# Softmax sums of three head pairs collected in one PSUM bank, one reciprocal for the three, and a new order of calls

## The chip, the core and the metric

The kernel runs on one core of a Trainium2 chip. The metric is the device time of one execution in microseconds (us): the median of several runs, 689.25 us for the kernel before.

## The reference

Attention with rotary positions, followed by a gated feed-forward layer, all in fp32:

```python
def _attn_ref(q, k, v):                      # 4 batches, 8 heads, 576 positions, 64 wide
    ...
    scores = scale * np.matmul(q_rot, k_rot.transpose(0, 1, 3, 2))
    scores = scores - np.max(scores, axis=-1, keepdims=True)
    attn = np.exp(scores)
    attn = attn / (np.sum(attn, axis=-1, keepdims=True) + 1e-09)
    return np.matmul(attn, v).astype(np.float32)

def _moe_ref(x, w_gate, w_val, w_out):       # 2304 x 512, 512 x 1536 twice, 1536 x 512
    gate = 1.0 / (1.0 + np.exp(-(x @ w_gate)))
    val = x @ w_val
    return (gate * val @ w_out).astype(np.float32)
```

`x` is the attention's output with the heads side by side. The feed-forward weights arrive as 64-bit floats.

## The kernel before

**Tiling.** The 8 heads of a batch go in 4 pairs (128 partitions), the 576 query positions of a batch in two halves of 256 and 320 (`HALVES`). A half of a batch passes through attention, then through `hidden` (12 blocks f of the hidden width; line 922 holds its matmuls, which need the attention output `xt` of all four pairs) and then `project` (line 958). fp32 numbers are mostly carried as two fp16 numbers, a high part and a remainder; a scale goes with each.

**Preparation.** At the start the weights are decoded from 64-bit words: `w_in_chunk` for 12 chunks (two exponent and low-bit steps, lines 476 to 484, a join on VectorE, line 488, then high parts and remainders; for six chunks, `VIA_PE`, TensorE makes the remainders with a scaled identity, line 529), and `w_out_decode` and `w_out_split` for the output weights. `values0_split` splits the values of batch 0.

**Batch 0, first half.** This half of 256 queries has its own path, for which the change is made. `keys_queries` turns q and k: TensorE multiplies by a 128x128 constant `turned` (line 639; it lies in the first quarter of the buffer `obuf[1]`), VectorE does the rest (lines 641 to 646). `front` computes scores directly, takes their row maxima (line 771) and brings these into row form. `back` then computes the scores transposed, with keys on the partitions, in five blocks j; ScalarE takes the exponential (line 818). `weigh` (line 822) multiplies, for each j and each of the two heads, the exponentials by the raw fp32 values into the single PSUM bank `v_ps` ("pv") and by a block of ones into a bank of the pool m ("sums"), so that each of the 64 rows of a head holds that head's sums; line 830 is the matmul of both. The end of `back`, per pair, is:

```python
op("ACT", ..., [U], [K], lambda E: A.activation(t(), sums()[:, 0:n], AF.Copy, bias=1e-9))      # line 839
op("DVE", ..., [], [K], lambda E: V.reciprocal(t(), t()))                                      # line 840
op("DVE", ..., ["pv"], [K], lambda E: V.tensor_tensor(                                         # line 841
    out=t(), in0=v_ps[:, 0:n], in1=t(), op=ALU.mult))
```

followed by a high part on ScalarE (line 464), a remainder (line 470) and a maximum (line 845) on VectorE.

**Pools.** PSUM holds two double banks s for scores, the bank pv, and three banks m. SBUF has three buffers p32, three th (the hidden blocks use them) and two p16.

**The order.** `Plan` collects every operation with a rank, an engine or several possible ones, and what it reads and writes; `order` plays it through with its own cost functions and, on each engine, takes the ready operation of the lowest rank; `emit` writes the instructions in that order. Nothing is decided on the chip. Operations enter through 269 calls (`at`), and three tables have one entry per call: `SHIFT` is added to the ranks of a call, `LEAD` to those of its loads, and `SIDE` places its movable operations (`alt`, line 401; `high`, line 407): 0 puts all on their first engine, 1 each first of two on the second engine, 2 all. High parts and low-bit decodes go to ScalarE or VectorE; the rope's two full-width steps per pair of batch 0 to VectorE or GpSimd, the six smaller ones per pair of later batches to GpSimd or VectorE.

## Time and profile before

| | us |
|---|---|
| median of 3 runs (lowest, highest) | 689.25 (688.71, 689.66) |
| the profiled execution | 686.14 |
| its span (first to last instruction) | 684.3 |
| TensorE matmul busy in the span | 645.9 (94%) |
| VectorE busy | 536.8 (78%) |
| ScalarE busy | 391.1 (57%) |
| GpSimd busy | 35.5 (5%) |

Busy shares are averages over stages with different limits. In the first stage, some 110 us, weights are decoded and batch 0 is prepared; later the hidden and output matmuls fill TensorE while the attention of the next batch runs beside them.

### The profile page before, as it was taken

The numbers are of one execution on the slowest core, as the hardware profiler recorded it, in microseconds if no ns is written. First come the engines' busy times: TensorE is split into PE (matmuls) and PEld (weight loads), VectorE is DVE, ScalarE is ACT, GpSimd is POOL, SyncE is SP. The second block draws the span as 40 slices with busy tenths as digits, with TensorE's granted clock in tenths as the row PEclk, the third lists the DMA queues.
The fourth block names the chain that finished last, engine by engine and source line by source line (L and its number), as shares of the span: only waits on it lengthen the run. The fifth ranks groups of instructions, "written<-read, shape, count | busy, mean of one in ns | idle before, by whom it ended". The sixth has DMA issues, their size and how long they took to land.

```text
span 684.3 us, 13000 instructions
## 1 busy us (share of the span) xinstructions
PE 645.9 (94%) x4922; PEld 428.7 (63%) x4922; DVE 536.8 (78%) x1306; ACT 391.1 (57%) x825; POOL 35.5 (5%) x33
## 2 busy tenths in 40 slices
PE   4798978999899999999999999999999999999997
PEld 2444546775466756886776555677885568767645
DVE  4999989999999998899998997597887774543200
ACT  4988889787746576665665545334545662612210
POOL 0000000001011010300001312000000000000000
PEclk9999999999999999999999999999999999999999
DMA  9854437898886588699367798422536661400010
GB/s 351 340 188 149 159 124 179 195 232 195 179 207 130 99 206 192 137 175 212 88 138 180 172 217 188 128 66 58 96 87 114 152 125 32 102 1 1 1 44 33
DMA packets 172669, 97.11 MB, mean 142 GB/s; under 512 B 152896, under 2 KB 161600, under 8 KB 170816
## 3 DMA queue, kind: packets, MB, share of 16 engines
q1 hardware_dynamic: 172608, 96.29, 57.2%
q8 instruction: 38, 0.62, 0.4%
q14 instruction: 23, 0.19, 0.1%
HBM read 40.83 MB, written 4.72 MB: 67 GB/s over the span
## 4 chain that ended last, share of the span: by engine, by line
PE 45%; DVE 30%; DMA 14%; issue 6%; ACT 3%; SPq 1%; POOL 1%; DVEq 0%; ACTq 0%; POOLq 0%
PE m L922 26%; PE m L958 9%; DMA pt<-p 7%; DVE p L470 6%; PE pv L871 4%; DVE p L737 4%; PE s L714 4%; DVE wo L488 2%; DMA stk<-sw 2%; DMA qk<-in_qk_dram 1%; DVE p L466 1%; DVE m L771 1%; DMA xt<-in_v_dram 1%; DVE gt L470 1%; DVE p L840 1%
## 5 line engine op out<-in xcount | busy, mean ns | idle before, releaser
L922 PE MATMUL m<-xt,w 128*128 128x256 f16 (+1 forms) x2304 | 294.8, 286 | 1.2 <-ACT xt L464 0.9
L922 PEld LDWEIGHTS <-w 128*128 128x128 f16 x2304 | 222.9, 98 | 63.7 <-issue 7.7
L958 PE MATMUL m<-wo,gt 128*128 128x512 f16 (+1 forms) x684 | 147.1, 368 | 1.1 <-DVE wo L470 1.1
L742 ACT ACTIVATE p<-p,st 128x576 f32<-128x576 f32 x128 | 98.7, 771 | 60.5 <-DVE p L737 53.4
L470 DVE SCALAR_TENSOR_TENSOR p<-p,st,p 128x576 f16<-128x576 f32 x128 | 107.1, 864 | 14.3 <-ACT p L464 13.9
L958 PEld LDWEIGHTS <-gt 128*128 128x128 f16 x684 | 66.0, 98 | 69.1 <-issue 4.3
L928 ACT ACTIVATE th<-m,gsc 128x320 f32<-128x320 f32 (+1 forms) x96 | 47.3, 494 | 82.2 <-PE m L922 78.6
L737 DVE TENSOR_SCALAR_CACHE_REDUCE p<-s,q_e 128x576 f32<-128x576 f32 x108 | 86.4, 810 | 4.1 <-PE s L714 3.6
L932 DVE SCALAR_TENSOR_TENSOR th<-th,m 128x320 f32<-128x320 f32 (+1 forms) x96 | 42.9, 448 | 39.8 <-PE m L922 38.5
L464 ACT ACTIVATE p<-p,st 128x576 f16<-128x576 f32 x91 | 66.9, 764 | 12.4 <-DMA pt<-p 6.7
L714 PE MATMUL s<-stk 128*128 128x288 f16 (+1 forms) x480 | 66.1, 287 | 4.5 <-DVE p L737 4.4
L871 PE MATMUL pv<-pt,v 128*64 128x320 f16 (+3 forms) x840 | 60.9, 290 | 2.1 <-DMA pt<-p 2.1
L714 PEld LDWEIGHTS <-stk 128*128 128x128 f16 (+1 forms) x480 | 41.5, 100 | 23.6 <-issue 12.0
L871 PEld LDWEIGHTS <-v 128*64 128x64 f16 (+1 forms) x840 | 43.3, 109 | 19.9 <-issue 16.2
L470 DVE SCALAR_TENSOR_TENSOR gt<-th,c_s,gt 128x320 f16<-128x320 f32 (+1 forms) x96 | 49.0, 512 | 8.0 <-ACT gt L464 7.3
L464 ACT ACTIVATE gt<-th,c_s 128x256 f16<-128x256 f32 (+1 forms) x50 | 26.1, 523 | 33.5 <-DVE th L932 29.1
L464 ACT ACTIVATE o<-m,o_s 128x512 f32<-128x512 f32 (+1 forms) x17 | 11.2, 657 | 37.4 <-PE m L958 37.3
L652 POOL TENSOR_TENSOR qk<-qk,tab 128x576 f32<-128x576 f32 x7 | 11.3, 1621 | 279.4 <-DMA qk<-in_qk_dram 209.1
L742 ACT ACTIVATION_READ_ACCUMULATOR p<-p,st 128x1 f32 x128 | 23.9, 187 | 0.0
L466 DVE TENSOR_SCALAR p<-p,st 128x576 f16<-128x576 f32 x37 | 21.0, 576 | 3.8 <-DMA pt<-p 3.5
L464 ACT ACTIVATE xt<-pv 128x320 f16<-128x320 f32 (+1 forms) x28 | 11.3, 405 | 21.2 <-PE pv L871 21.1
L663 ACT ACTIVATE sink<-qk 128x576 int8<-128x576 f32 x24 | 16.3, 680 | 11.8 <-DVE qk L656 5.6
(146 smaller groups left out, 652.3 us busy)
## 6 DMA issues: line engine op xcount, KB each, us to landing
wo<-in_w_dram SPq DMA_DIRECT2D x11, 1024.0 KB, 4.9
qk<-in_qk_dram SPq DMA_DIRECT2D x12, 576.0 KB, 5.5
sw<-in_qk_dram SPq DMA_DIRECT2D x12, 576.0 KB, 4.2
xt<-in_wo_dram SPq DMA_DIRECT2D x12, 512.0 KB, 3.8
stk<-sw SPq DMA_DIRECT2D x24, 216.0 KB, 3.6
stk<-sw SPq DMA_DIRECT2D x72, 72.0 KB, 2.8
out_dram<-o SPq DMA_DIRECT2D x15, 256.0 KB, 2.6
xt<-in_v_dram SPq DMA_DIRECT2D x3, 1152.0 KB, 7.3
```

Source lines behind the costliest of these rows:

```text
L464: A.activation(o, src, AF.Copy, scale=scale)
L466: E.tensor_scalar(out=o, in0=src, scalar1=scale, scalar2=1.0, op0=ALU.mult, op1=ALU.mult)
L470: V.scalar_tensor_tensor(out=o, in0=src, scalar=scale, in1=hi, op0=ALU.mult, op1=ALU.subtract)
L663: op("ACT", c_act(S) + 0.09, rank, [X[m]], ["sink", M], lambda E, m=m: A.activation(sink, x[:, m], AF.Abs, accum_out=q_m[:, k, m:m + 1]))
L714: T.matmul(o[:, c, 0:288], lhsT=q[:, rows:rows + width], rhs=kk[:, c * 288:c * 288 + 288], start=(m == 0), stop=(m == 1))
L737: lambda E, h=h, c=c: V.tensor_scalar(out=prs[c]().rearrange("p (c n) -> p c n", c=2), in0=h()[:, :, 0:288], scalar1=down, scalar2=None, o ...
L742: lambda E, c=c: A.activation(prs[c](), prs[c](), AF.Exp, bias=st[:, k, 0, c:c + 1], scale=-1.0, accum_out=st[:, k, 1, c:c + 1]))
L871: T.matmul(v_ps[64 * e:64 * e + 64, 0:n], lhsT=v16[hs, p, a, g, :], rhs=pt[z][hs, c * 9 + g, 0:n], start=(first and m == 0), stop=(last an ...
L922: T.matmul(m()[:, 0:n], lhsT=w16[:, f, g, a, cc, :], rhs=x[:, cc, c, c0:c0 + n], start=(k == 0), stop=(k == 11))
L928: op("ACT", c_act(n), rank - 0.05, [m, ("gsc", b, f)], [r], lambda E, m=m: A.activation(t(), m()[:, 0:n], AF.Tanh, scale=gsc[:, b, f:f + 1]))
L932: op("DVE", c_dve(n, psum=True), rank - 0.05, [m], [r], lambda E, m=m: V.scalar_tensor_tensor(out=t(), in0=t(), scalar=1.0, in1=m()[:, 0:n ...
L958: T.matmul(m()[:, 0:w], lhsT=gt[:, f, a, c0:c0 + 128], rhs=wo16[:, f, x, c:c + w], start=(f == 0 and k == 0), stop=(f == NF - 1 and k == 2))
```

## The change

`back` gets groups: the pairs 0, 1 and 2 of the first half form one, pair 3 stands alone and keeps the old ending. In the group, the three pairs' sums go into the same bank: the block of ones is replaced by a 64-column window of `hot` (zeros with one column of ones, in the second quarter of `obuf[1]`), so that pair p's sums land on row p of each head's 64 rows. Each pair's product in pv is copied by ScalarE into a th buffer. After the third pair the bank is copied once and its reciprocal taken once; then, per pair, two fp32 matmuls with a broadcast column of the identity spread the pair's row over 64 rows in a bank of m, VectorE multiplies the copy by it, and the split and maximum follow as before (`split`; its high part may now go to VectorE, but all the calls concerned have side 0). `front` and `back` also learn the second half, which `ACROSS = ()` leaves unused.

The cut diff:

```diff
+ACROSS = ()
+GROUPS = ((0, (0, 1, 2)), (0, (3,)))
...
+    hot = obuf[1][:, 128:256]
...
-    def front(p, z, rank):
+    def front(p, i, z, rank):
...
+    groups = {}
+
+    def back(p, i, z, rank):
 
         kT, qT = qk0[p][:, 0], qk0[p][:, 1]
         R = [("stk", m) for m in range(8 * p, 8 * p + 8)] + [("mr", z), ("obuf", 0)]
-        n = HALVES[0][1]
-        w = p % 2
+        c0, n = HALVES[i]
+        w = i or p % 2
         pp = pT[w]
-        sums, U = m_place()
+        pairs = next(g for h, g in GROUPS if h == i and p in g)
+        G = groups.setdefault((i, pairs), {"left": len(pairs), "raw": {}})
+        first = G["left"] == len(pairs)
+        G["left"] -= 1
+        last = not G["left"]
+        if first:
+            G["sums"] = m_place()
+        sums, U = G["sums"]
+        alone = len(pairs) == 1
...
-                        T.matmul(o[es, 0:n], lhsT=ones[hs, 0:64] if one else early[hs, 3 * p + g // 3, 64 * (g % 3):64 * (g % 3) + 64],
-                                 rhs=pp[hs, at0:at0 + n], start=(j == 0), stop=(j == 4), skip_group_check=True)
+                        w_t = early[hs, 3 * p + g // 3, 64 * (g % 3):64 * (g % 3) + 64]
+                        if one:
+                            w_t = ones[hs, 0:64] if alone else hot[hs, 63 - p:127 - p]
+                        T.matmul(o[es, 0:n], lhsT=w_t, rhs=pp[hs, at0:at0 + n], start=(j == 0 and (first or not one)),
+                                 stop=(j == 4 and (last or not one)), skip_group_check=True)
         for js in ((0, 1), (2, 3, 4)):
-            mm(len(js) * 0.0035 * n, rank - 0.02, [("pt", w, j) for j in js] + [("v32", p)], ["pv", U],
+            mm(len(js) * 0.0035 * n, rank - 0.02, [("pt", w, j) for j in js] + [("v32", p), ("obuf", 1)], ["pv", U],
                lambda js=js: weigh(js), mode="C")
-        K = lease("p32")
+
+        def split(p, t, T0):
+            x = xt[0][:, p, :, c0:c0 + n]
+            X, Z = ("xt", 0, p, i), ("xm", 0, i)
+            high(n, rank - 0.02, [T0, ("vs", 0)], [X], x[:, 0], t, v_s[:, 0:1])
+            op2(c_dve(n, two=True), rank - 0.02, [T0, ("vs", 0)], [X], lambda E: rest(x[:, 1], t(), v_s[:, 0:1], x[:, 0]))
+            op("DVE", c_dve(n), rank, [X], [Z], lambda E: V.tensor_reduce(
+                out=xm[:, 0, i, p:p + 1], in_=x[:, 0], axis=AX.X, op=ALU.max, apply_absolute_value=True))
+        K = lease("p32") if last else None
         t = lambda: K()[:, 0:n]
-        x = xt[0][:, p, :, 0:n]
-        X, Z = ("xt", 0, p, 0), ("xm", 0, 0)
-        op("ACT", c_act(n) - 0.11, rank - 0.02, [U], [K], lambda E: A.activation(t(), sums()[:, 0:n], AF.Copy, bias=1e-9))
-        op("DVE", 0.1 + 0.0061 * n, rank - 0.02, [], [K], lambda E: V.reciprocal(t(), t()))
-        op("DVE", c_dve(n, psum=True), rank - 0.02, ["pv"], [K], lambda E: V.tensor_tensor(
-            out=t(), in0=v_ps[:, 0:n], in1=t(), op=ALU.mult))
-        op("ACT", c_act(n), rank - 0.02, [K, ("vs", 0)], [X], lambda E: scaled(A, x[:, 0], t(), v_s[:, 0:1]))
-        op2(c_dve(n, two=True), rank - 0.02, [K, ("vs", 0)], [X], lambda E: rest(x[:, 1], t(), v_s[:, 0:1], x[:, 0]))
-        op("DVE", c_dve(n), rank, [X], [Z], lambda E: V.tensor_reduce(
-            out=xm[:, 0, 0, p:p + 1], in_=x[:, 0], axis=AX.X, op=ALU.max, apply_absolute_value=True))
+        if last:
+            op("ACT", c_act(n) - 0.11, rank - 0.02, [U], [K], lambda E: A.activation(t(), sums()[:, 0:n], AF.Copy, bias=1e-9))
+            op("DVE", 0.1 + 0.0061 * n, rank - 0.02, [], [K], lambda E: V.reciprocal(t(), t()))
+        if alone:
+            op("DVE", c_dve(n, psum=True), rank - 0.02, ["pv"], [K], lambda E: V.tensor_tensor(
+                out=t(), in0=v_ps[:, 0:n], in1=t(), op=ALU.mult))
+            split(p, t, K)
+            return
+        raw = G["raw"][p] = lease("th")
+        op("ACT", c_act(n) - 0.11, rank - 0.03, ["pv"], [raw], lambda E: A.activation(raw()[:, 0:n], v_ps[:, 0:n], AF.Copy))
+        if last:
+            for q in pairs:
+                f, F = m_place()
+                r = G["raw"][q]
+                def spread(f=f, q=q):
+                    for e in range(2):
+                        T.matmul(f()[64 * e:64 * e + 64, 0:n], lhsT=ident[:, 64 * e + q:64 * e + q + 1].to_broadcast([128, 64]),
+                                 rhs=t(), start=True, stop=True)
+                mm(0.00175 * n, rank - 0.02, [K, "ident"], [F], spread, mode="C")
+                op("DVE", c_dve(n, psum=True), rank - 0.02, [F], [r], lambda E, f=f, r=r: V.tensor_tensor(
+                    out=r()[:, 0:n], in0=f()[:, 0:n], in1=r()[:, 0:n], op=ALU.mult))
+                split(q, lambda r=r: r()[:, 0:n], r)
...
+        G.memset(hot, 0.0)
+        G.memset(hot[:, 63:64], 1.0)
...
-            for k, g in ((0, front(p, p % 2, t)), (1, back(p, p % 2, t + step))):
+            for k, g in ((0, front(p, 0, p % 2, t)), (1, back(p, 0, p % 2, t + step))):
```

The tables `SHIFT`, `SIDE` and `LEAD` are replaced as a whole; their 269 calls are the same. The sides that change among the calls of batch 0 and batch 1, with the operations that change engine:

| call | side | moves |
|---|---|---|
| keys_queries batch 0, pair 1 | 0 to 1 | first rope step, the multiply of 1,152 columns, VectorE to GpSimd |
| values0_split pair 2 | 1 to 0 | high part, VectorE to ScalarE |
| w_in_chunk 0 | 0 to 2 | two half-size low-bit decodes, two high parts, two scaled identities to VectorE |
| w_in_chunk 1 | 1 to 2 | a high part and a scaled identity to VectorE |
| w_in_chunk 4, 10 | 1 to 2 | a high part each to VectorE |
| w_in_chunk 5 | 1 to 0 | low-bit decode and a high part to ScalarE |
| w_in_chunk 9 | 0 to 1 | low-bit decode and a high part to VectorE |
| w_in_chunk 11 | 2 to 1 | a high part to ScalarE |
| w_out_decode 0, 10, 11 / 8 | 0 to 1 / 1 to 0 | low-bit decode (512 columns) to VectorE / ScalarE |
| w_out_split 0, 7, 8 / 3, 5 | 0 to 1 / 1 to 0 | high part to VectorE / ScalarE |
| attention of batch 1 | several | 8 high parts to VectorE, 7 to ScalarE |

In batch 2, eight high parts net of the attention and two of the values move from ScalarE to VectorE, in batch 3 three net of the attention to VectorE and four of the values to ScalarE; rope work of the pairs moves both ways. By the ranks of the loads SyncE issues weight chunk 2, `turned` and the identity, then the tables and pair 0's q and k; before, it was chunk 2, the tables, pair 0's q and k, `turned`, the identity. The last call in rank is `project` of batch 3, tile 3 (before, tile 1).

## Rows read from the trace of the kernel before

**Rows 1.** PE, PEld, DVE, ACT, POOL busy us by stretch; then granted clock, DMA share, GB/s.

```profile
0.00:10.00 10.00, 1.18 (x3) 0.93 (x4) 1.92 (x2) 4.45 (x9) 1.21 (x12) 1.00 0.82 315
...
40.00:110.00 70.00, 60.27 (x428) 32.58 (x429) 68.14 (x168) 61.65 (x133) 0.00 (x0) 0.98 0.49 166
110.00:200.00 90.00, 84.45 (x656) 56.45 (x654) 86.96 (x222) 68.57 (x151) 7.43 (x4) 1.00 0.87 198
200.00:400.00 200.00, 196.78 (x1628) 136.72 (x1627) 187.29 (x460) 121.32 (x260) 21.61 (x15) 1.00 0.74 162
400.00:680.70 280.70, 278.38 (x2129) 189.25 (x2127) 165.71 (x410) 110.97 (x227) 5.28 (x3) 1.00 0.36 81
```

**Rows 2.** The chain that ended last, 60 to 104 us: start us, us, what.

```profile
65.72 1.66 DVE p L840
...
67.98 0.61 DVE wo L481
...
77.65 0.40 DVE w L466
78.05 1.66 DVE p L840
...
88.95 1.66 DVE p L840
...
92.21 0.95 PE pv L830 x4
...
94.01 0.85 PE pv L830 x4
...
96.71 0.43 PE pv L830 x4
...
99.05 1.75 DVE p L840
```

**Rows 3.** Waits of TensorE and VectorE, 40 to 110 us: total us, times, longest.

```profile
PE pv L830 <- DVE p L841: 1.6, 2, 1.3
...
DVE p L840 <- ACT p L839: 1.8, 1, 1.8
```

**Rows 4.** The stretches around pair 3's sums, columns as above.

```profile
90.00:92.00 2.00, 0.94 (x8) 0.39 (x4) 2.00 (x5) 1.40 (x4) 0.00 (x0) 1.00 0.74 301
...
93.00:94.00 1.00, 1.00 (x8) 0.62 (x6) 1.00 (x3) 1.00 (x3) 0.00 (x0) 0.50 0.00 0
```

**Rows 5.** Groups by line, 0 to 110 us: busy us, mean ns | idle before.

```profile
L464 ACT ACTIVATE w<-wo,w_s 128x512 f16<-128x512 f32 x15 | 11.1, 771 | 2.3 <-DVE w_s L432 2.0 <-DVE vm L591 0.3
...
L839 ACT ACTIVATE p<-m 128x256 f32<-128x256 f32 x4 | 1.5, 382 | 1.7 <-PE m L830 1.7
...
L644 DVE TENSOR_TENSOR stk<-stk,tab 128x1152 f32<-128x1152 f32 x4 | 5.4, 1348 | 0.0
...
L466 DVE TENSOR_SCALAR v<-gt,v_s 128x576 f16<-128x576 f32 x3 | 2.3, 802 | 0.0
...
L470 DVE SCALAR_TENSOR_TENSOR p<-p,st,p 128x576 f16<-128x576 f32 x2 | 1.6, 810 | 0.0
...
L466 DVE TENSOR_SCALAR ids<-ident,w_s 128x128 f32<-128x128 f32 x4 | 1.0, 253 | 0.0
```

**Rows 6.** Timeline of TensorE and SyncE, one row each.

```profile
97.50 0.19 PEld L830 LDWEIGHTS pv<-pt,gt 64*64 64x64 f32 x4 [0.39 <-issue]
...
2.84 0.44 SPq L996 DMA_DIRECT2D ident<-in_const_dram  x1
```

**Rows 7.** Timeline of GpSimd and of VectorE, around 163 us.

```profile
162.76 2.34 POOL L654 TENSOR_TENSOR sw<-sw,tab 128x576 f32<-128x576 f32 x1 [18.44 <-DMA sw<-in_qk_dram]
...
205.01 1.40 POOL L654 TENSOR_TENSOR sw<-sw,tab 128x576 f32<-128x576 f32 x1 [15.04 <-DMA sw<-in_qk_dram]
...
163.75 1.96 DVE L470 SCALAR_TENSOR_TENSOR p<-p,st,p 128x576 f16<-128x576 f32 x1
```

**Rows 8.** Group of the attention splits on VectorE, 200 to 400 us, columns as in rows 5.

```profile
L466 DVE TENSOR_SCALAR p<-p,st 128x576 f16<-128x576 f32 x18 | 9.9, 556 | 0.4 <-DMA pt<-p 0.4
```

More of the change, by code (lines that the diff above doesn't have):

```diff
@@ L760, in front @@
         M = ("m2", z)
[L761 to L762 removed]
+        for x, t in enumerate(((0, 1), (2, 3, 4))[i]):
+            for c in range(2 if t < 4 else 1):
                 k = lease("s")
                 def direct(t=t, c=c, k=k):
[L766 to L772 removed]
+                    for cc in ((c,) if t < 4 else (0, 1)):
+                        for e in range(2):
+                            hs = slice(64 * e, 64 * e + 64)
+                            w = 128 if t < 4 else 64
+                            o = k()[:, e, 0:288] if t < 4 else k()[hs, cc, 0:288]
+                            T.matmul(o, lhsT=qT[hs, 128 * t:128 * t + w], rhs=kT[hs, 288 * cc:288 * cc + 288],
+                                     start=True, stop=True)
+                mm(0.48, rank, R, [k], direct, mode="R" if t < 4 else "Q")
+                o = m2[:, z, x, c] if t < 4 else m2[:, z, x, :, 0]
+                op("DVE", c_dve(S, psum=True), rank - 0.01, [k], [M], lambda E, k=k, o=o: V.tensor_reduce(
+                    out=o, in_=k()[:, :, 0:288], axis=AX.X, op=ALU.max))
                 yield
[L774 to L775 removed]
+        q = 3 if i else 2
+        a, b, c = (cb[:, z, 0:q, :, r] for r in range(3))
+        y = mx[:, z, 0:q]
         W = [M, ("cb", z)]
[L777 removed]
+        tiny(rank - 0.01, [], W, lambda: V.tensor_tensor(out=y, in0=m2[:, z, 0:q, 0], in1=m2[:, z, 0:q, 1], op=ALU.max), port=True)
         tiny(rank - 0.01, [], W, lambda: V.tensor_copy(a, y), port=True)
@@ L787, in turn_up @@
                          start=True, stop=True)
-        n = HALVES[0][1]
-        mm(0.3, rank - 0.02, [("cb", z), "nid"], [Z], turn_up)
+            for e in range(2 * i):
+                hs = slice(64 * e, 64 * e + 64)
+                T.matmul(ps()[hs, 256:320], lhsT=cb[hs, z, 2, 0], rhs=nid[hs, hs], start=True, stop=True)
+        n = HALVES[i][1]
+        mm(0.3 + 0.3 * i, rank - 0.02, [("cb", z), "nid"], [Z], turn_up)
         op("ACT", c_act(n) - 0.11, rank - 0.02, [Z], [("mr", z)], lambda E: A.activation(mr[z][:, 0:n], ps()[:, 0:n], AF.Copy))
-    def back(p, z, rank):
+    groups = {}
+    def back(p, i, z, rank):
         kT, qT = qk0[p][:, 0], qk0[p][:, 1]
         R = [("stk", m) for m in range(8 * p, 8 * p + 8)] + [("mr", z), ("obuf", 0)]
-        n = HALVES[0][1]
-        w = p % 2
+        c0, n = HALVES[i]
+        w = i or p % 2
         pp = pT[w]
-        sums, U = m_place()
+        pairs = next(g for h, g in GROUPS if h == i and p in g)
[7 more added lines that the diff above has]
+        alone = len(pairs) == 1
         for j in range(5):
@@ L811, in across @@
                     keys = slice(64 * e + 128 * j, 64 * e + 128 * j + 128) if j < 4 else (slice(512, 576), slice(0, 64))[e]
-                    T.matmul(o, lhsT=kT[hs, keys], rhs=qT[hs, 0:n], start=False, stop=True)
+                    T.matmul(o, lhsT=kT[hs, keys], rhs=qT[hs, c0:c0 + n], start=False, stop=True)
             mm(0.00215 * n, rank, R, [k], across, mode="R" if j < 4 else "Q")
@@ L1034, in attend0_rest @@
             t = lo + p * step
+            if p in ACROSS:
+                for k, g in ((0, front(p, 1, p % 2, t)), (0.5, back(p, 1, p % 2, t + 0.5 * step))):
+                    for n in range(6):
+                        at(t + step * (k + n / 12), next, g, None)
+                continue
             at(t - 0.4 * step, values0_split, p, t - 0.4 * step)
```

13 lines of the change are left out of this document (1 added, 12 removed), and 68 rows, old and new, of tables (LEAD, SHIFT, SIDE).

## The prediction, made before the changed kernel was run

> **What bounds the kernel now.** I read the stretches first. From 400 us to the last matmul TensorE does nothing but work, and from 200 to 400 us it is idle for 3.2 us of 200, so a gain has to come from the time before. There TensorE idles 9.7 us of the 70 from 40 to 110 and 5.5 of the 90 from 110 to 200, while VectorE is busy 68.1 of 70 and 87.0 of 90 [rows 1]. VectorE's queue sets the pace of the first 110 us, and ScalarE (61.7 of 70) is close behind.
>
> The chain of waits says what is in that queue. All four reciprocals of batch 0's first half lie on it: 1.66 us for each of pairs 0 to 2 and 1.75 for pair 3, 6.7 us together [rows 2]. Then, at 92.21, the chain leaves VectorE: the weighing matmuls of pair 3 (line 830) had to wait until pair 2's product (line 841) had emptied the single bank pv, and line 841 stands behind pair 2's reciprocal. TensorE lost 1.6 us in two such waits [rows 3]. Worse, after that idling its granted clock is 0.50, the lower of its two levels (1.2 GHz), from 93 to 94 us [rows 4], and each step of pair 3's weighing takes 0.85 us where the later ones take 0.43 [rows 2]. VectorE in turn idles 1.8 us before the last reciprocal, waiting for pair 3's sums [rows 3]. So pair 3 is the gate: no hidden matmul of batch 0 can finish before its product.
>
> **The change part by part.** *Reciprocals.* Of four, two go (pairs 0 to 2 share one). On the queue each costs what the chain gives it, so 2 x 1.66 = **-3.3 us** of VectorE. The three products stay, from a PSUM bank times SBUF as before.
>
> *The bank pv.* It is now emptied by a ScalarE copy of the size of line 839's, 0.38 us [rows 5], and no longer by a product that waits for a reciprocal. Pair 3's weighing need not wait for pair 2's reciprocal: **-1.6 us** of wait. With that idling gone I also expect the higher clock: four steps at 0.85 instead of 0.43 cost 4 x 0.42 = **-1.7 us**. ScalarE gets three such copies and loses two of line 839's, +0.38 us net, which I cost at nothing because it loses far more below; without that cover it is 0.38.
>
> *The spread.* Three times two fp32 matmuls of 256 columns, each pair like one step of line 830, 0.43 us: 1.3 us, and entering the mode once costs 0.39 us of issue [rows 6]; 1.7 in all. It is nothing if they fall into the 9.7 us in which TensorE idles, 1.7 if they stand in front of pair 3's weighing or the hidden matmuls. I take **+0.4**, the entry alone, as the rows nearest to it show TensorE idle 1.06 of 2 us just before 92 [rows 4]. A bank of the pool m is held from pair 0's first weighing to pair 2's last, and three th buffers until the three products; nobody else needs th before pair 3 is done, and the bank is costed in a rival.
>
> *The start.* GpSimd sets two more small memsets, and SyncE now issues both 64 KB constants ahead of the tables and the first q and k, which TensorE's first work waits for; before, ident came after all of these [rows 6]. 64 KB at 315 GB/s [rows 1] is **+0.2 us**. Should SyncE wait for the memsets, the queue still has the 1 MB weight chunk to move meanwhile.
>
> *The sides.* The table of sides moves work between engines, and here the change takes back much of what it gives. Priced by queue time (a row's duration less the 0.08 by which it overlaps with the next: 1.66 for the reciprocal's 1.74), up to the gate: the weight chunks bring VectorE two half-size bit decodes (0.35 each, estimated as somewhat over half of a whole one's 0.61), five high parts net (0.40 each) and three scaled identities (0.18 each, from 253 ns), and one whole decode comes for one that goes [rows 2, 5]: 0.7 + 2.0 + 0.5 = +3.2. One w_out decode: +0.35. One value split leaves (802 ns): -0.7. One rope multiply of 1,152 columns leaves for GpSimd (1,348 ns): -1.3 [rows 5]. With the reciprocals VectorE's queue stands at -3.3 + 3.2 + 0.35 - 0.7 - 1.3 = **-1.7 us** up to the gate, and it has 1.8 us of idling to give besides. ScalarE loses 0.77 us with each high part [rows 5], for five of them 3.9.
>
> A GpSimd multiply is not free for VectorE. At 163.75 an operation of VectorE with two SBUF inputs, issued while GpSimd multiplied, took 1.96 us instead of 0.81 [rows 5, 7]. GpSimd needed 1.40 to 2.34 us for 576 columns [rows 7], so 2.8 to 4.7 for 1,152 is my estimate. I take no cost, since VectorE has reductions and products from PSUM in its queue then, and keep the other end for a rival. The Trainium skill, GPSIMD Engine Reference, section Specifications, says that GpSimd shares its SBUF interfaces with VectorE and contends with its two-input instructions; by that rule the -1.3 could become a loss, and row 163.75 agrees.
>
> *After the gate.* Two w_out decodes in and one out (+0.35), three high parts of w_out in and two out and one of the last weight chunk out (0), one attention split more in batch 1 (+0.45): 0.8 us on a VectorE that has 3.0 us idle in 90 [rows 1]. Between 0 and 0.8 I take **+0.4**.
>
> *The order.* All 269 calls get new shifts. Which instruction follows which can't be read off the table, so it gets no term; its bounds are the 5.5 us that TensorE still idles from 110 to 200 and, on the other side, as much new idling as VectorE's tightest stretch allows.
>
> **The sum.** The gate comes earlier by the smaller of two: VectorE can give 1.7 + 1.8 = 3.5, TensorE's side of pair 3 gives 1.6 + 1.7 = 3.3. So -3.3 + 0.4 + 0.2 + 0.4 = **-2.3 us**. The profiled execution took 686.14 us (span 684.3 and 1.84 around it), 3.1 less than the median of the runs, 689.25; I expect a profiled execution of 683.8 and a median of **687.0**. What a measurement can tell from no change is 0.2%, 1.4 us.
>
> **Rivals.** *More than that.* The order fills TensorE's idling from 110 to 200 as well: half to all of 5.5 us on top, 681.5 to 684.3. For it: ScalarE, the second tightest engine, is relieved by about 4 us. Against: VectorE is busy 97% there and gets 0.8 us more. 0.18.
>
> *Nothing measurable.* Pair 3 gets its early start, but the three products, splits and maxima of pairs 0 to 2 now come in one burst behind a chain of copy, reciprocal, spread and product, and that burst, with the bank of m held throughout, becomes the gate. Then only VectorE's -1.7 counts, against 1.7 for the spread, 0.2 and 0.4: +0.6, 689.9; within the bound it covers 687.9 to 690.6. 0.18.
>
> *Slower, by VectorE in batch 2.* The sides of batch 2 bring VectorE ten splits of 576 columns net (eight in the attention, two of the values) at 0.56 us [rows 8], 5.6 us, into 200 to 400 us, where VectorE is busy 187 of 200 and TensorE idles only 3.2 [rows 1]. It decides once more than 3.7 us of the 5.6 become idling of TensorE: 690.6 to 692.6 (687.0 + 5.6). Against: VectorE still has 12.7 us free there. 0.10.
>
> *Slower, by GpSimd's multiply.* If everything in VectorE's queue then has two SBUF inputs, VectorE stands for 2.8 to 4.7 us and the -1.3 is lost too. The gate is then set by VectorE: -3.5 + 1.3 + 2.8 to 4.7 = +0.6 to +2.5, and with 1.0 for the other terms 690.9 to 692.8. The Trainium skill's rule of the GPSIMD Engine Reference is this rival's. 0.07.
>
> **Chances and range.** The forecast has 0.47, from 684.3 to 687.9. Faster by over 0.2%: 0.47 + 0.18 = 0.65. Within it 0.18. Slower 0.10 + 0.07 = 0.17. The range runs from 682.8, which leaves out about a third of the first rival, to 690.8, which leaves out most of the two slower ones.
>
> **What would show it.** Right: two RECIPROCALs of 256 columns instead of four, the first at the end of pair 2; no wait of line 830's successor on a VectorE product; a granted clock of 1.0 throughout 85 to 100 us; the first complete hidden group about 3 us earlier; the span shorter by about 2. Wrong: pair 3's weighing waits for something else (a bank of m, its exponentials), the low clock returns, TensorE idles more between 200 and 400 us, or VectorE's two-input operations stretch beside GpSimd near the start.

## The result, and the profile after

The changed kernel takes 679.01 us (median of 4 runs, 678.08 to 680.9); the kernel before, beside it on the same chip, 688.98. The ratio of the two kernels over their runs is 0.9872, 95% interval 0.9826 to 0.9917, or 8.8 us; the medians alone differ by 10.0. The forecast, 687.0 with a range down to 682.8, had the sign and missed the size by a factor of more than three. The profiled execution took 679.09 us, span 677.3: 7.0 us less span than before.

The stretches of the changed kernel answer to [rows 1] (same columns):

```profile
0.00:10.00 10.00, 0.66 (x2) 0.55 (x3) 1.92 (x2) 4.42 (x9) 1.45 (x14) 1.00 0.83 302
...
40.00:110.00 70.00, 63.94 (x464) 35.92 (x463) 68.20 (x174) 59.73 (x125) 0.00 (x0) 0.98 0.46 159
110.00:200.00 90.00, 85.37 (x650) 55.92 (x648) 84.49 (x224) 66.92 (x148) 4.23 (x3) 0.98 0.86 189
200.00:400.00 200.00, 199.75 (x1618) 136.47 (x1615) 189.11 (x459) 114.08 (x251) 21.89 (x13) 1.00 0.71 162
400.00:677.30 277.30, 273.86 (x2131) 188.04 (x2127) 169.61 (x423) 111.90 (x230) 12.15 (x8) 1.00 0.39 87
```

From 40 to 110 us TensorE idles 6.1 us instead of 9.7, and from 200 to 400 us 0.25 instead of 3.2. In the first of these stretches VectorE is as busy as before (68.20 against 68.14 of 70) and ScalarE has 1.9 us less. (Rows 1 end at TensorE's last matmul, the last row here at the end of the span.) The difference of the two spans can be split at 200 us. The stretch from there to the end, kernel before:

```profile
200.00:684.30 484.30, 475.17 (x3755) 325.96 (x3753) 353.00 (x869) 232.77 (x488) 26.89 (x17) 1.00 0.52 114
```

Changed kernel:

```profile
200.00:677.30 477.30, 473.61 (x3745) 324.51 (x3742) 358.72 (x882) 225.98 (x480) 34.03 (x21) 1.00 0.52 119
```

TensorE has 475.17 us of work left at 200 us before and 473.61 after: the changed kernel has a **lead of 1.6 us** there. Behind 200 us it idles 484.30 - 475.17 = 9.1 us before and 477.30 - 473.61 = 3.7 us after: **5.4 us less**. Together 7.0. These waits of the kernel before (TensorE's, 200 to 681 us) are what went; the same view of the changed kernel from 200 us to its end is empty:

```profile
PE pv L871 <- DMA pt<-p: 2.1, 3, 1.3
PE s L714 <- DVE p L737: 1.9, 3, 0.8
PE pv L446 <- DVE row L443: 1.1, 2, 0.6
PE pv L441 <- DVE xm L886: 0.2, 1, 0.2
```

How much went before 200 us and how much after is not the same in every profile of the new order. In that of e6 below, which differs from the changed kernel by one early multiply and takes 0.8 us more by the medians, the lead is 2.2 us and the idle time behind 200 us is 3.3 us less than before; there one of these waits is back:

```profile
PE s L722 <- DVE p L745: 2.0, 4, 0.6
```

The gate, TensorE's timeline of the changed kernel (start us, us, what, idle before it in brackets), answers to the chain of [rows 2]:

```profile
89.48 0.65 PE L854 MATMUL pv<-pt,gt 128*64 128x256 f32 x4
...
91.26 1.03 PE L885 MATMUL m<-p,ident 128*64 128x256 f32 x8
92.12 0.60 PE L854 MATMUL pv<-pt,gt 128*64 128x256 f32 x4
...
94.96 0.65 PE L885 MATMUL m<-p,ident 128*64 128x256 f32 x4
95.54 1.24 PE L706 MATMUL s<-stk 64*128 64x288 f32 x8
98.96 0.57 PE L456 MATMUL m<-w_m,ones 128*128 128x3 f32 x2 [2.17 <-ACT w L515]
99.39 4.25 PE L966 MATMUL m<-xt,w 128*128 128x256 f16 x24
...
105.35 1.48 PE L966 MATMUL m<-xt,w 128*128 128x256 f16 x12
```

Its stretches there (columns as in [rows 1]; the last three are granted clock, DMA share, GB/s):

```profile
84.00:92.00 8.00, 7.97 (x72) 4.55 (x70) 7.67 (x14) 7.11 (x17) 0.00 (x0) 1.00 0.70 263
92.00:98.00 6.00, 4.78 (x40) 2.42 (x36) 6.00 (x13) 5.40 (x14) 0.00 (x0) 1.00 0.53 158
...
99.00:102.00 3.00, 3.00 (x15) 2.25 (x16) 2.98 (x12) 2.34 (x6) 0.00 (x0) 0.50 0.53 172
```

Pair 3's weighing starts at 89.48 instead of 92.21, at the high clock and without the wait of [rows 3]. The first hidden group (12 matmuls, one half of a block f; the expectations below call it the first hidden block) starts at 99.39 and runs on into the second, where the kernel before stopped for 0.9 us in the midst of its first group. But TensorE now waits 2.17 us for ScalarE (line 515, a weight's high part), and the low clock that was at 93 [rows 4] is at 99 to 102. The third hidden group starts at 105.35; in the kernel before, it is

```profile
109.20 5.42 PE L922 MATMUL m<-xt,w 128*128 128x256 f16 x48
```

So at that point the lead is 3.9 us, of which 1.6 are left at 200. One piece of the loss can be read: from 140 to 144 us the changed kernel has the low clock once more, behind waits of 0.37, 0.20 and 0.39 us, and the kernel before has not. Four us at 0.58 are worth 2.3 at the high clock, 1.7 us lost. Changed kernel, then the kernel before:

```profile
140.00:144.00 4.00, 4.00 (x21) 2.13 (x20) 4.00 (x12) 3.26 (x8) 0.00 (x0) 0.58 1.14 251
```

```profile
140.00:144.00 4.00, 4.00 (x41) 3.20 (x38) 4.00 (x8) 3.20 (x9) 1.28 (x1) 1.00 0.94 239
```

The reciprocals (line, engine, ns least/median/most, first and last start):

```profile
L871 DVE RECIPROCAL p<-p x2: 1740/1746/1753, 88.8 to 96.0; 128x256 f32<-128x256 f32 x2
```

### The profile page after: what moved, and what is told of

Same layout as the page of the kernel before. It is cut to its first block, busy times and chain, and to the rows that moved or that the text cites. A ratio compares the mean times of both kernels' runs of the same rounds, so it can differ in the third digit from the quotient of the medians.

```text
span 677.3 us, 13009 instructions
## 1 busy us (share of the span) xinstructions
PE 649.1 (96%) x4934; PEld 430.2 (64%) x4934; DVE 539.1 (80%) x1323; ACT 378.9 (56%) x803; POOL 42.4 (6%) x39
## 4 chain that ended last, share of the span: by engine, by line
PE 65%; DVE 21%; DMA 8%; ACT 3%; issue 3%; SPq 0%; DVEq 0%; ACTq 0%
PE m L966 31%; PE m L1002 18%; PE pv L915 6%; PE s L717 6%; DVE p L740 4%; DVE p L473 3%; DMA qk<-in_qk_dram 2%; DMA stk<-in_qk_dram 2%; DVE wo L491 1%; DMA pt<-p 1%; DVE gt L473 1%; DMA xt<-in_wo_dram 1%; DVE th L976 1%; DMA p<-p 1%; DMA wo<-in_w_dram 1%
## 5 line engine op out<-in xcount | busy, mean ns | idle before, releaser
L966 PE MATMUL m<-xt,w 128*128 128x320 f16 (+1 forms) x2304 | 296.8, 287 | 1.1 <-ACT th L972 0.8
L473 DVE SCALAR_TENSOR_TENSOR p<-p,st,p 128x576 f16<-128x576 f32 x128 | 103.1, 832 | 5.3 <-ACT p L467 4.8
L972 ACT ACTIVATE th<-m,gsc 128x256 f32<-128x256 f32 (+1 forms) x96 | 47.3, 493 | 58.4 <-PE m L966 57.9
L976 DVE SCALAR_TENSOR_TENSOR th<-th,m 128x256 f32<-128x256 f32 (+1 forms) x96 | 42.8, 446 | 34.0 <-PE m L966 33.4
L467 ACT ACTIVATE p<-p,st 128x576 f16<-128x576 f32 x79 | 58.2, 765 | 15.0 <-DVE st L751 4.2
L473 DVE SCALAR_TENSOR_TENSOR gt<-th,c_s,gt 128x256 f16<-128x256 f32 (+1 forms) x96 | 50.5, 530 | 8.9 <-ACT gt L467 8.2
L467 ACT ACTIVATE gt<-th,c_s 128x320 f16<-128x320 f32 (+1 forms) x47 | 24.5, 530 | 28.6 <-DVE th L976 28.0
L469 DVE TENSOR_SCALAR p<-p,st 128x576 f16<-128x576 f32 x49 | 25.1, 525 | 3.3 <-DMA pt<-p 2.9
```

The source lines that it names most:

```text
L467: A.activation(o, src, AF.Copy, scale=scale)
L469: E.tensor_scalar(out=o, in0=src, scalar1=scale, scalar2=1.0, op0=ALU.mult, op1=ALU.mult)
L473: V.scalar_tensor_tensor(out=o, in0=src, scalar=scale, in1=hi, op0=ALU.mult, op1=ALU.subtract)
L966: T.matmul(m()[:, 0:n], lhsT=w16[:, f, g, a, cc, :], rhs=x[:, cc, c, c0:c0 + n], start=(k == 0), stop=(k == 11))
L972: op("ACT", c_act(n), rank - 0.05, [m, ("gsc", b, f)], [r], lambda E, m=m: A.activation(t(), m()[:, 0:n], AF.Tanh, scale=gsc[:, b, f:f + 1]))
L976: op("DVE", c_dve(n, psum=True), rank - 0.05, [m], [r], lambda E, m=m: V.scalar_tensor_tensor(out=t(), in0=t(), scalar=1.0, in1=m()[:, 0:n ...
```

## The experiments

Ratios are to the kernel before, run beside each on the same chip. The changed kernel itself stands only beside the run of the result; the kernel before had medians from 686.5 to 689.0 us in the different groups of runs, so a difference in us between two groups is good to some 2 us, and two ratios whose intervals overlap are not told apart. "Order kept" means that the plan was made with the unchanged costs and the edit put in only while the instructions were written, so that every engine's other instructions stand in the order of the named kernel. The first four runs do not keep it: there the planner orders everything anew.

### Halves of the change, planned anew

*e1: the group with the old tables.* `SHIFT`, `SIDE` and `LEAD` are those of the kernel before.

> The changed code with the three tables of the kernel before: the sums of three pairs in one bank, one reciprocal, spread by TensorE, but the old shifts, sides and leads. Theory A (gate plus late waits: the group brings the gate some 3 us forward, the new order removes TensorE's waits after 200 us besides): 2 to 4 us faster than before, 685 to 687 against 689, and TensorE still waits some 3 to 5 us after 200 us. Theory B (the order alone): no faster than before, within 1.4 us. Theory C (the group only pays with an order searched for it): no faster or slower here, and the other half-change is no faster either.

Measured: 694.59 us, ratio 1.0111 (1.0075 to 1.0146).

*e2: the new tables without the group.*

```diff
-GROUPS = ((0, (0, 1, 2)), (0, (3,)))
+GROUPS = ((0, (0,)), (0, (1,)), (0, (2,)), (0, (3,)))
```

> The changed code with the new tables, but each pair its own group, so four reciprocals, no spread, the old ending of each pair. Theory A: slower than the changed kernel by what the group gives, 2 to 4 us (681 to 683), faster than before by 6 or more. Theory B: as the changed kernel, 678 to 680. Theory C: 686 or more.

Measured: 701.52 us, 1.0227 (1.0181 to 1.0273).

*e3 and e4: the tables cut in two*, one half for the weights and batch 0, the other for batches 1 to 3; e3 takes the new first half and the old second, e4 the reverse.

> The changed code; the calls of batch 0 and of the weights have the new tables, the calls of batches 1 to 3 the old ones. Theory A: the gate stays early, the waits of TensorE after 200 us come back: 4 to 6 us slower than the changed kernel, 683 to 685. If the gain was all made before 110 us: as the changed kernel, within 1.4 us.

> The changed code; the calls of batch 0 and of the weights have the old tables, the calls of batches 1 to 3 the new ones. Theory A: 2 to 5 us slower than the changed kernel, 681 to 684, with the few waits of TensorE after 200 us still gone. If the gain was all made in the first stage by the new order: as before, 688 to 690.

Measured: e3 712.67 us, 1.0363 (1.033 to 1.0396); e4 701.96 us, 1.0211 (1.0177 to 1.0244). All four are slower than both kernels, as theory C of the first two has it. e4's output is wrong besides, from a cause that wasn't sought, so its time says least. TensorE's longest wait in e3, 200 to 400 us:

```profile
PE s L717 <- DVE p L740: 13.0, 6, 4.1
```

Each table seems to fit the code and the costs that it was made for; with others the plan is worse. Since everything is ordered anew, such halves don't say what a part is worth, and the other runs keep the order.

### One thing taken from the changed kernel, order kept

*e5: the time of two reciprocals given back to VectorE.* Three reciprocals of 80 columns of a spare buffer behind the ScalarE copy of pair 0 and of pair 1.

```diff
+        if not last:
+            P.then[len(P.tasks) - 1] = lambda: [V.reciprocal(idle, idle) for _ in range(3)]
```

> The changed kernel with every engine's order kept, and two costs put back: where ScalarE copies pv for pair 0 and for pair 1, VectorE takes three reciprocals of 80 columns of a spare buffer (three times some 0.56 us of queue time, 1.7 for the 1.66 of one reciprocal of 256). Theory A (VectorE's queue sets the pace up to the gate): 2.5 to 3.4 us slower, 681.5 to 682.5. Rival (the reciprocals were hidden, what counted was the bank pv and the order): less than 1.4 us slower.

Measured: 685.5 us, ratio 0.9975 (0.9952 to 0.9997): 6.5 us more than the changed kernel, beyond both expectations. The six instructions:

```profile
L883 DVE RECIPROCAL idle<-idle x6: 644/652/654, 67.6 to 77.4; 128x80 f32<-128x80 f32 x6
```

Six at 0.652 less the overlap of 0.08 are 3.4 us of queue. TensorE's waits from 62 to 110 us show where they grow; the second is new:

```profile
PE m L459 <- ACT w L518: 5.0, 4, 2.0
PE m L797 <- DVE cb L792: 2.3, 1, 2.3
```

TensorE's weight loads stand 5.0 us behind those of the changed kernel at 100 us (the n-th against the n-th), 4.6 at 200 and 6.6 at the end. The granted clock has a part in it: its mean from 40 to 110 us is 0.95, in the changed kernel 0.98, and 0.03 of 70 us is 2 us, estimated from these two means and at most.

*e6: pair 1's rope multiply back on VectorE.*

```diff
+            if p == 1:
+                k = P.tasks[-1]
+                P.tasks[-1] = k[:2] + (lambda _: V.tensor_tensor(out=x, in0=x, in1=cos, op=ALU.mult),) + k[3:]
```

> The changed kernel with every other instruction in its order, and pair 1's rope multiply of 1,152 columns back from GpSimd to VectorE, at the same place in time. If the move was a gain: 0.5 to 1.3 us slower, 679.5 to 680.3. If GpSimd's multiply held VectorE's two-input operations: the same or up to 1.5 us faster, 677.5 to 679.0.

Measured: 679.83 us, 0.9883 (0.9861 to 0.9905). The move to GpSimd is worth 0.8 us by the medians, or nothing; no cost of it can be seen.

*e10: the six short reciprocals of e5 put into batch 2's attention instead.*

```diff
+        if (b, i) == (2, 0) and p in (1, 2):
+            P.then[len(P.tasks) - 1] = lambda: [V.reciprocal(idle, idle) for _ in range(3)]
```

> The changed kernel, order kept, with the same six short reciprocals as in e5_two_more_recips (3.4 us of VectorE) but placed in the attention of batch 2, at some 250 and 290 us, where VectorE is busy 95% and TensorE idles 0.25 us of 200. If VectorE's time is dear only up to the gate: within 1 us of the changed kernel, 679 to 680. If VectorE sets the pace there too: +3.4 to +6.5, 682.4 to 685.5.

Measured: 682.45 us (678.27 to 685.41), 0.9915 (0.9881 to 0.9949). They fell later than I had written, at 374.5 to 406.3 us, and cost 3.4 us by the medians for 3.4 of queue; the interval overlaps that of the changed kernel, so the cost is not resolved. TensorE's longest wait there, 300 to 400 us:

```profile
PE s L720 <- DVE p L743: 2.6, 4, 1.0
```

*e11 and e12: the old sides, order kept.* Each movable operation is issued on the engine that the old table gives it: in e11 those of batches 2 and 3, in e12 those of the weights and of batch 0 (e13 to e16 use the same edit).

```diff
+        o = places[int(P.other > (P.alts - 1) % 2)][0]
+        if o != e:
+            k = P.tasks[-1]
+            P.tasks[-1] = k[:2] + (lambda _: fn(eng.get(o)),) + k[3:]
```

> The changed kernel, order kept, with the movable operations of batches 2 and 3 on the engines of the kernel before (VectorE gives splits back to ScalarE and the rope's multiplies go back). If the new sides took away TensorE's waits after 200 us: +2 to +5, 681 to 684, with TensorE idle 2 us or more from 200 to 400 us. If these waits went by the order alone, the sides a matter of taste: within 1 us, 679 to 680.

> The changed kernel, order kept, with the movable operations of the weights and of batch 0 on the engines of the kernel before: VectorE gets lighter by about ten operations up to 200 us, ScalarE heavier by as many. Theory S: time saved on VectorE is worth only what is handed on to ScalarE, whose queue releases VectorE's next work; then the changed kernel loses most of its gain, +3 to +6, 682 to 685, and ScalarE's busy time from 40 to 110 us rises by 4 us or more. Rival O: the order alone spends the saving, and the sides are within 1 us: 678 to 680. The forecast's pricing (VectorE's queue counts one for one) would make it faster: 676 to 678.

Measured: e11 680.71 us, 0.9889 (0.9863 to 0.9915); e12 685.73 us, 0.9975 (0.9953 to 0.9996). By the medians the late sides are worth 1.7 us, which the intervals don't resolve, and the early ones 6.7, which they do, although the old ones make VectorE's queue *lighter* (in e12 63.73 us from 40 to 110 instead of 68.20). As in e5, the mean clock of that stretch is 0.95. In e12 VectorE waits; its two longest waits from 40 to 110 us:

```profile
DVE row L462 <- PE pv L460: 1.6, 1, 1.6
DVE w L489 <- ACT w L483: 1.6, 2, 1.1
```

ScalarE's busy time rose by only 1.1 us there (60.87 of 70), not by the 4 that I had expected: other ScalarE work moved out of the stretch, and from 110 to 200 us it is busy 4.7 us more.

### The forecast's terms in the old order

*e7: the bank pv emptied by a ScalarE copy*, four reciprocals, order of the kernel before.

```diff
+        raw = th[p % 3][:, 0:n]
+        P.then[len(P.tasks) - 1] = lambda: A.activation(raw, v_ps[:, 0:n], AF.Copy)
-            out=t(), in0=v_ps[:, 0:n], in1=t(), op=ALU.mult))
+            out=t(), in0=raw, in1=t(), op=ALU.mult))
```

> The kernel before with every engine's order kept; only pv is emptied by a ScalarE copy into a th buffer right behind the copy of the sums, and the product reads that buffer. All four reciprocals stay. If the wait on pv and the low clock behind it were worth what the prediction said: 1.6 to 3.3 us faster than before. If VectorE's queue alone was the bound: within 1.4 us, as four more ScalarE copies are nothing and the reciprocals are still there.

Measured: 685.77 us, 0.9976 (0.9957 to 0.9994). No product is waited for any more, but pair 3's weighing still has the low clock. TensorE stood idle 1.87 us just ahead of it, for the exponentials of ScalarE; that wait was there in the kernel before too, with 1.54 us. Timeline and stretch:

```profile
90.33 1.24 PE L705 MATMUL s<-stk 64*128 64x288 f32 x8 [1.87 <-ACT pt L820]
```

```profile
92.00:94.00 2.00, 2.00 (x12) 1.14 (x10) 2.00 (x7) 2.00 (x5) 0.00 (x0) 0.50 0.01 4
```

*e8: two reciprocals' time taken away*, and *e9: this and the copy of e7*.

```diff
+        if p < 2:
+            k = P.tasks[-1]
+            P.tasks[-1] = k[:2] + (lambda _: V.reciprocal(idle, idle),) + k[3:]
```

> The kernel before, every engine's order kept, but the reciprocals of pairs 0 and 1 taken over 8 columns of a spare buffer (so their sums are not inverted): two reciprocals' time leaves VectorE's queue, as the forecast priced it, and nothing else changes. If VectorE's time up to the gate counts one for one, as the forecast had it: -3.3 us, 683.8 against 687.1. If the order of the kernel before takes such a saving back in later waits: 0 to -1.5. If a us of VectorE is worth two, as the reciprocals added to the changed kernel showed (+6.5 for 3.4): -6.

> As e8_short_recips, and the bank pv is emptied by a ScalarE copy as in e7_before_pv_copied: both terms of the forecast together, in the old order. The forecast's gate: -3.3 (the smaller of two sides), at most -4.9 if e7's -1.6 adds to e8's -3.3. If it comes out at -8, the group without any new order explains the whole gain; if at -3 to -5, the rest of the -8 is the new order's.

Measured: e8 687.25 us, **0.9999** (0.997 to 1.0027); e9 687.01 us, 0.9989 (0.9967 to 1.0011). Both terms of the forecast, and nothing gained that these intervals resolve: e8's allows a gain of 2.1 us and e9's one of 2.3, less than the 3.3 of the forecast. For e8 the chain of waits shows where the first saving goes: where the kernel before had the reciprocal of pair 0 at 65.72 [rows 2], the chain now runs through ScalarE.

```profile
62.67 1.14 DVE wo L491
...
63.84 0.77 ACT w L515 x2
64.60 0.27 ACT p L842
64.87 0.65 ACT w L515 x2
...
66.27 1.06 ACT wo L479
...
67.68 0.54 ACT xt L467
...
68.24 0.48 DVE xt L473
```

VectorE reaches pair 0's remainder at 68.24, in the chain of the kernel before at 68.73: of 1.66 us, 0.5 is left, as the high part before it stands in ScalarE's queue. e9 gets further. TensorE's timeline:

```profile
94.87 0.60 PE L833 MATMUL m<-pt,ones 64*64 64x256 f32 x4
...
97.66 1.14 PE L931 MATMUL m<-xt,w 128*128 128x256 f16 x9
100.51 0.27 PE L931 MATMUL m<-xt,w 128*128 128x256 f16 x1 [1.71 <-ACT xt L467]
...
102.50 0.59 PE L444 MATMUL pv<-ident,xm 128*1 128x128 f32 x2 [1.07 <-DVE xm L895]
103.02 2.19 PE L706 MATMUL s<-stk 64*64 64x288 f32 x8
...
105.64 2.65 PE L931 MATMUL m<-xt,w 128*128 128x256 f16 x12
```

Its stretches:

```profile
92.00:98.00 6.00, 5.90 (x46) 3.35 (x43) 5.56 (x13) 6.00 (x16) 0.00 (x0) 1.00 0.30 94
98.00:101.00 3.00, 1.07 (x9) 0.67 (x7) 2.91 (x10) 3.00 (x10) 0.00 (x0) 1.00 0.51 173
101.00:108.00 7.00, 5.90 (x26) 3.08 (x25) 6.18 (x18) 7.00 (x17) 0.00 (x0) 0.52 0.65 177
```

Up to 97.66 all goes as forecast: no wait for pv, the high clock from 92 to 98, pair 3's last weighing step at 94.87 (97.98 in the kernel before), the first hidden matmul at 97.66 (99.92). Then the first group waits 1.71 us for ScalarE's high part, 0.25 for a remainder and 1.07 for a maximum, the clock falls to its lower level, and from 101 to 108 us matmuls take twice as long (the second group 2.65 us, a group in the changed kernel at 105.35 only 1.48). The third group starts at 109.40, in the kernel before at 109.20: the lead is gone.

*e13, e14, e16: the new sides of the weights and of batch 0 in the old order*: alone (e13), with both terms (e14), and as e14 but with the rope left on VectorE (e16).

> The kernel before, order and reciprocals kept, with the movable operations of the weights and of batch 0 on the engines of the changed kernel: VectorE about ten operations heavier. The forecast's pricing: +3 (690). Theory S: ScalarE's relief is worth something but VectorE has no room for it: 0 to +2, 687 to 689. Rival O: within 1 us, or a little slower.

> The kernel of e9 (order of the kernel before, two reciprocals taken over 8 columns of a spare buffer so that two pairs' sums are not inverted, the bank emptied by a copy) with the engines of e13 besides: VectorE's saving is handed on to ScalarE without any new order. Theory S: 3 to 6 us faster than the kernel before, 681 to 684. Rival O: no faster than e9, 686 to 688, since only the new order can spend the saving.

> As e14_short_copied_sides (old order, two reciprocals over 8 columns, the bank emptied by a copy, the changed kernel's engines for the weights and batch 0), but pair 1's rope multiply stays on VectorE: e14 was 4.1 us behind by 40 us, where its TensorE waited for that multiply on GpSimd. If the multiply on GpSimd hid a gain of the other sides: 681 to 685. If the new sides are worth nothing in the old order: 686 to 688, as e9.

Measured: e13 691.0 us, 1.0064 (1.0041 to 1.0088); e14 690.81 us, 1.0046 (1.0026 to 1.0065); e16 690.3 us, 1.0043 (1.0026 to 1.0061). In the old order the new sides cost some 3 to 4 us, with the terms (against e9) and without. So my theory that VectorE's saving pays once it is handed on to ScalarE found no support. It isn't refuted either, since all three runs have a long stretch of low clock at the gate, as e9 has; the same sides with the clock kept weren't tried. In e16:

```profile
108.00:114.00 6.00, 5.61 (x28) 3.17 (x26) 4.84 (x16) 6.00 (x15) 0.00 (x0) 0.54 0.62 145
```

*e17: e9 with TensorE kept busy* in the waits of the first hidden group, by 10 and 6 idle matmuls (their results are never read) into unused columns of pv; *e18: e7 with the same* (5, 5, and 5 more ahead of pair 3's weighing), so with all four reciprocals and the full result, where e17, like e9, leaves the sums of pairs 0 and 1 uninverted.

```diff
+    def fill(n):
+        for _ in range(n):
+            T.matmul(v_ps[:, 384:512], lhsT=ones, rhs=ones, start=True, stop=True)
...
+                if first and k == 9:
+                    fill(10)
```

> As e9_short_and_copied (two pairs' sums not inverted), with 10 and 6 idle matmuls of 128 columns at the two waits of the first hidden block (98.8 to 102.5 us in e9), behind which e9's clock was 0.50 for 6.8 us and its lead of some 3 us was lost. If the low clock alone gave the lead back: 3 us faster than the kernel before, 683 to 684.5. If VectorE and ScalarE, behind in the same order, take it back in later waits: 685.5 to 687.

> The kernel before with the bank emptied by a copy (e7) and TensorE kept busy by idle matmuls in its three waits around the gate (5 ahead of pair 3's weighing, 5 and 5 at the waits of the first hidden block), so that the granted clock stays high; all four reciprocals stay. It differs from e17 (680.7) by the two reciprocals. If these are worth the forecast's 3.3 once the clock is kept: 683.5 to 684.5. If keeping the clock is the whole of e17's gain: 680 to 681.5. If the clock is low anyway, at another place: 685.5 to 687.

Measured: e17 **680.72 us, 0.9892 (0.9871 to 0.9913)**; e18 **682.08 us, 0.992 (0.9892 to 0.9947)**. The stretch of e17 beside that of e9:

```profile
98.00:101.00 3.00, 3.00 (x29) 2.91 (x29) 2.91 (x8) 3.00 (x8) 0.00 (x0) 1.00 0.54 180
101.00:108.00 7.00, 6.43 (x51) 4.49 (x51) 7.00 (x25) 7.00 (x17) 0.00 (x0) 1.00 0.64 174
```

Of e18:

```profile
101.00:108.00 7.00, 5.84 (x45) 4.06 (x44) 7.00 (x22) 7.00 (x18) 0.00 (x0) 1.00 0.58 164
```

The clock stays at its higher level and e9's missing gain is there: 6.3 us less than e9, without any new order, and about twice the 3 us that I had expected. In the two profiles, 6.1 us apart, 2.9 us are lead at 200 us and 3.2 are idle time that goes after it. e18 against e7 gains 3.7 us from 15 idle matmuls, which lies between the values expected. What the two reciprocals add once the clock is kept (e17 against e18, 1.4 us by the medians) isn't resolved, as the intervals overlap.

*e15: the same at the changed kernel's gate*, 12 idle matmuls in the wait of 2.17 us at 96.8.

> The changed kernel, order kept, with 12 idle matmuls of 128 columns put where TensorE waits 2.2 us for ScalarE just ahead of the first hidden matmuls (96.8 to 99.0 us), after which the granted clock is 0.50 for a while and the first 24 hidden matmuls take 4.25 us instead of 2.8. If the low clock follows from that idling: 1.0 to 1.5 us faster, 677.5 to 678. If the low clock comes anyway, or its loss is waited out by VectorE behind it: no change, 679. If the fillers outlast the wait: up to 1 us slower.

Measured: 681.72 us (680.09 to 684.47), 0.9911 (0.9888 to 0.9935): not faster. The first two hidden groups now keep the high clock, but the fillers outlast the wait by 0.3 us (the next matmul at 99.28), the first group then waits 0.5 us for a remainder, and the scores behind it come only 0.3 us earlier (103.54 against 103.87), which is lost again by 200 us (473.6 us of work left in both). By the medians it is 2.7 us slower than the changed kernel, but the intervals overlap. No run beats the changed kernel.

### Where the time lies, run by run

From each profile: TensorE's work left at 200 us, and its idle time from there to the end of the span.

| run | order | work left | idle after |
|---|---|---|---|
| before | old | 475.2 | 9.1 |
| e7 copy | old | 474.3 | 8.7 |
| e8 short reciprocals | old | 473.9 | 9.3 |
| e9 both | old | 475.8 | 9.3 |
| e13 new sides | old | 479.7 | 9.5 |
| e14 both, new sides | old | 481.9 | 9.4 |
| e16 both, new sides but the rope's | old | 481.2 | 8.1 |
| e17 both, clock kept | old | 472.9 | 6.1 |
| e18 copy, clock kept | old | 472.5 | 6.3 |
| after | new | 473.6 | 3.7 |
| e6 rope multiply back | new | 473.0 | 5.9 |
| e15 changed kernel, fillers | new | 473.6 | 6.8 |
| e10 reciprocals' time, later | new | 474.2 | 6.3 |
| e5 reciprocals' time back | new | 478.4 | 5.6 |
| e12 old early sides | new | 479.4 | 5.3 |
| e11 old late sides | new | 474.1 | 5.6 |

All seven profiles in the new order idle less after 200 us than the old order without fillers, 3.7 to 6.8 us against 8.1 to 9.5, even those that come there 3 to 4 us later than the kernel before (e5, e12: 5.3 to 5.6). So some 2 to 4 us go with the new order, whichever engines the early (e12) or the late (e11) operations have; all seven have the group too, so order and group aren't told apart here. The changed kernel's own 3.7 is the least of the seven, and a single profile. A lead takes some idle time away as well: e17 and e18, 2.3 and 2.6 us ahead of the kernel before at 200 us, idle 6.1 and 6.3 in the old order.

## Why the prediction was right and wrong

**What bounds the kernel.** Here the step failed: "From 400 us to the last matmul TensorE does nothing but work, and from 200 to 400 us it is idle for 3.2 us of 200, so a gain has to come from the time before." The last row of [rows 1] itself has 278.38 of 280.70 us busy, so 2.3 us were there, and with the 3.2 they are 5.5: the waits listed above. Of the 7.0 us of span gained, 5.4 lie where the forecast had excluded a gain; in e6's profile it is 3.3 of 5.5. Either way it is more than half.

**The order.** "It gets no term; its bounds are the 5.5 us that TensorE still idles from 110 to 200." That nothing can be read off the table is true, but the bound was the wrong stretch: there 4.6 us of the 5.5 are still idle. The bound should have been all idle time behind the gate. The rival *More than that* (0.18) had the mechanism, in the wrong place and with 681.5 at best too small.

**The gate, -3.3, and the sum, -2.3.** The lead at 200 us is 1.6 us (2.2 in e6), so the sum was of the right size for the time up to there, but by luck: its terms were not sound one by one. The sign "the first complete hidden group about 3 us earlier" didn't come either; that group ends at 102.11 instead of 102.95; only the next is far earlier, 103.63 instead of 108.08. *Reciprocals -3.3*: two of 256 columns are left, the first at the end of pair 2, as forecast; but the price "what the chain gives it" is 0.0 where it is taken away in the old order (e8, at most 2.1 by its interval), and 6.5 where 3.4 us are added in the new one (e5). *The bank pv -1.6*: the wait went, and e7's 0.24% is 1.6 us (0.4 to 3.0 by its interval), though only 1.27 of the 1.6 stood at pair 3. *Low clock -1.7*: high through pair 3's weighing, as forecast, but the wait for pv was not its only source: in e7, without that wait, the clock there is 0.50 behind the wait for the exponentials, which the forecast passed over. In the changed kernel it isn't gone but stands some 6 us later, behind a wait for ScalarE. That it would follow the next wait is what the forecast lacked, and e17 and e18 show what it costs. The sign "a granted clock of 1.0 throughout 85 to 100 us" held to 99. The Trainium skill, TensorE: Matmul & The Clock Gate, section "HAM oscillation — how this bites in real kernels", tells of a kernel in which the waits between bursts of matmuls threw the clock back each time, and advises a loop order that keeps TensorE going. The trace agrees (0.52 from 101 to 108 us in e9 behind waits of 1.71, 0.25 and 1.07 us, 1.00 in e17, where idle matmuls fill them), with waits shorter than those of that kernel.

**The spread, +0.4.** It stands inside pair 3's weighing, on TensorE's path: two pairs keep it from 91.26 to 92.12, the third, alone, from 94.96 to 95.54, 1.4 us together, nearer to the upper end of 1.7. **The start, +0.2:** TensorE's busy time up to 10 us falls from 1.18 to 0.66, so about 0.5.

**The sides, -1.7 up to the gate.** VectorE's queue was priced, and ScalarE's relief (3.9 us) at nothing. e12 shows the price is not of one engine: with the old sides VectorE has less to do and the kernel is 6.7 us slower, of which the lower clock may be 2 us (estimated as for e5). That relief alone isn't a gain either, e13 shows. In e5 and e8 TensorE and VectorE wait for ScalarE behind a change of VectorE's work, so queue time summed over a stage of one engine is no price.

**The other rivals.** *Nothing measurable*: the burst of products did not become the gate; they run at 92.4, 93.3 and 95.7 us, ahead of pair 3's reciprocal at 96.0. *VectorE in batch 2* didn't come: VectorE is busy 189.1 of 200 and TensorE idles 0.25. Its pricing may have been right in kind: 3.4 us put there cost 3.4 by the medians (e10), not clear of noise. *GpSimd's multiply* had no cost that e6 shows. GpSimd's timeline:

```profile
22.59 2.67 POOL L647 TENSOR_TENSOR stk<-stk,tab 128x1152 f32<-128x1152 f32 x1 [20.55 <-PE s L642]
```

VectorE's beside it:

```profile
22.54 0.76 DVE L644 TENSOR_TENSOR sw<-s,tab 128x576 f32<-128x576 f32 x1 [0.21 <-PE s L642]
23.66 0.76 DVE L644 TENSOR_TENSOR sw<-s,tab 128x576 f32<-128x576 f32 x1 [0.36 <-PE s L642]
```

As the forecast supposed, VectorE then has products from PSUM, and they keep their 0.76 us (all eight of line 644 take 0.75 to 0.76). The Trainium skill's rule (GPSIMD Engine Reference, section Specifications) names VectorE instructions with two SBUF inputs or in a 2-port perf mode; these products have one input from PSUM, so the rule for two SBUF inputs was neither shown nor refuted here.

**What stays open.** The change gains without keeping the clock: its mean granted clock is 0.89 from 10 to 40 us (before 0.94), 0.98 from 40 to 110 (0.98) and 0.98 from 110 to 200 (1.00). How the gain splits between group, sides and order cannot be said, because they don't add: in the old order the terms give 0.1% (e9), in the new order without VectorE's saving the gain is 0.25% (e5), together 1.3%. With the clock kept, the terms give 1.1% in the old order (e17, two pairs' sums uninverted), so a new order is not the only way to such a gain. Which instruction of the new order takes which late wait away wasn't tried.

## What to carry to other kernels

In a kernel that an order written out by hand keeps full, time saved on one engine has no fixed price: keep every engine's order and take the saving away or double it before it is put into a sum, and bound a new order by all idle time behind the gate, however late and thin it lies. Where a wait comes just ahead of the matmuls that matter, look at the granted clock behind it: a handful of idle matmuls in that wait shows in one run what the low clock costs, here 6.3 us (e17 against e9), nearly as much as the whole change. They must not outlast the wait: in e15 they did by 0.3 us, and nothing was gained. Removing one wait can carry the low clock to the next, so follow the lead to the end of the span and not only past the gate.

## What the runs showed of the hardware that I had not expected

- Short waits with work between them were followed by the lower clock: behind 1.71, 0.25 and 1.07 us in e9, with three matmuls between, it was 0.52 for 7 us, and 1.00 in e17 with the first and the last of these waits filled. An idle matmul of 128x128 fp32 costs 0.22 us (10 in the 2.23 us from 98.91 to 101.14 in e17), so some 3.5 us of them bought 6.3.
- A RECIPROCAL's time grew by 6.2 to 6.3 ns per column: 0.200 us for 8 columns (e8), 0.652 for 80 (e5) and 1.746 for 256.
- Matmuls whose weights are one broadcast column of the identity took no longer than those with ordinary weights: the spread of two head pairs (line 885) took 0.86 us, 0.43 for each, as a step of the weighing.
